# Long convolution and spectral mixing on one core: the Z of both sequences of a tick copied out of PSUM in one instruction

## The chip, the cores and the metric

The kernel runs on one core of a Trainium2 chip. A core has TensorE (PE in the profile; its weight loads are the row PEld), VectorE (DVE), ScalarE (ACT), GpSimd (POOL) and SyncE (SP, which here only starts DMAs). Each takes its own instructions in their order, and they wait for one another on semaphores. The metric is the device time of one execution in microseconds. Three runs of the kernel before took 392.10, 393.78 and 391.25 us, median 392.1. One execution was also profiled; its span from the first to the last instruction is 390.0 us, and every time of a single instruction is from it.

## The reference

Two operations, one behind the other. The first is a long convolution of x (8 sequences of 5696 positions, 128 channels) with a filter h per channel, by a Fourier transform of double length. The second transforms the result along the sequence, keeps 64 modes, mixes the channels of each mode with a complex matrix, transforms back, adds, and applies a channel matrix with a ReLU:

```python
    Xf = np.fft.rfft(x, n=L, axis=1)              # L = 2 * S
    Hf = np.fft.rfft(h, n=L, axis=0)
    y = np.fft.irfft(Xf * Hf[None, :, :], n=L, axis=1)[:, :S, :]
    ...
    X = np.fft.rfft(x, axis=1)                    # x is the y above
    Yr = np.einsum('bmd,mde->bme', Xr, w_r) - np.einsum('bmd,mde->bme', Xi, w_i)
    Yi = np.einsum('bmd,mde->bme', Xr, w_i) + np.einsum('bmd,mde->bme', Xi, w_r)
    Y[:, :n_modes] = Yr + 1j * Yi
    y = np.fft.irfft(Y, n=S, axis=1)
    u = x + y
    return (u + np.maximum(u @ w_ch, 0.0)).astype(np.float32)
```

## The kernel before

**Stages.** The transform of length 2·5696 is split in two: first over 89 points (90 frequencies k), then over 64. The 8 sequences are worked on in 4 groups of two. For each group `a_tile` (32 tiles) makes the first transform, and PE's matmuls `ps<-F,Xin` are its rows. Then come the *ticks*: 23 of them, each with four frequencies k (the last with two), so four blocks of 128 channels, or 512 columns, for each of the two sequences. After the four groups a last part goes back to positions, mixes the modes and writes the output. In the profiled execution the ticks of group 0 take place at some 46 to 96 us, those of group 1 at 112 to 151, of group 2 at 167 to 207 and of group 3 at 222 to 265, with the first transforms between them; the last part fills the rest.

**One tick** (function `tick`) of group `g_` at time t has these steps, each for another tick's data:

- `second(g_, t)`: the transform over 64 points, 16 small matmuls (`ps<-As,M`), into two neighbouring PSUM banks, one per sequence. Two such pairs of banks, 0 and 1 or 2 and 3, take turns.
- `products(g_, t)`: the product with the filter's transform (tile Hs), on DVE, into one of three buffers U. As a rule ACT first copies both banks to SBUF as fp16 (`copied`, rows `Xs<-ps`, 1024 columns; two buffers), and DVE multiplies from there (`U<-Xs,Hs`). In a *straight* tick DVE reads PSUM itself (`U<-ps,Hs`) and ACT's copy falls away.
- Z of tick t − 2 (`LC` = 2): four matmuls of 512 columns (`ps<-U,Wc`), two for each sequence b, the second adding to the first in the same bank. Then ACT copies each bank to the fp16 tile Zs or Zt, with the two sequences interleaved block by block, and SP writes the tile to DRAM (`zscr<-Zs`).
- G of tick t − 3 (`LM` = 3): eight small matmuls that read Zs (`ps<-G,Zs`) and add up the 64 modes in bank 7.
- in group 0 alone `filter_tick(t + 6)`: 16 matmuls (`ps<-Ah,M`) for the filter's own transform into banks 2 and 3, a copy of them to Hs, and two DMAs by SP that swap the halves of its partitions (`Hs<-Hs`). The product six ticks later needs them.

**Order on PE.** In group 0 a tick is: second stage, Z, G, filter. In groups 1 to 3 ticks go in pairs, an odd t and the next even one (`twin`): the second stages of both, Z, G, then Z and G of the even tick. Ticks 0 to 2 are the start; the pairs are (1, 2), (3, 4) ... (21, 22), and Z is there from tick 2. The last Z's fall in ticks 23 and 24, which have no second stage. In groups 0 to 2 the first tiles of the next group's `a_tile` stand between the steps of ticks 22 to 25 (`border`); in group 3 nothing does. Copies of x to their place for the next group (`x_place`, row `Xin<-Xt` on DVE) and the loads for them (`x_load`, POOL) are also made in the ticks of groups 0 to 2.

**Order on ACT.** An Xs copy and the Z copies in turn, as the ticks name them. In a pair with a straight product it is Xs of the even tick, then the Z copies of both ticks behind one another.

**Who waits for whom.** The order of all instructions is the program's; a recorder (`R.add`) derives the waits from tokens. `("bank", i)` is one of them: a matmul into a bank waits for the copy that read it last, and a copy waits for the last matmul into each bank that it reads. A copy that reads two banks waits for both, and both are free only when it has ended. Z's banks are 4, 5 and 6 in turn (`ZBANK`, by `turns`), one per sequence: 4 and 5, 6 and 4, 5 and 6, and so on. The filter copy's engine is chosen in `filter_tick`: ACT for ticks 0 to 5 except 2, DVE else.

Of the kernel before, what the change touches and what calls it, by code (L numbers as in the profile page):

```python
# [4 lines left out]
P = 128  # L5
# [118 lines left out]
def bass_long_conv_fft__then__afno_spectral_mix_kernel(nc, x, h, moe_w_r, moe_w_i, moe_w_ch, out):  # L124
    B, S, D = x.shape
# [72 lines left out]
    zs = nc.dram_tensor("zscr", [NP * NK * P, 2 * D], F16, kind="Internal")  # L198
# [7 lines left out]
    def at(name, cols, dt, off):  # L206
        return nc.alloc_sbuf_tensor_at(name, [P, cols], dt, offset=off)
# [21 lines left out]
    NU, NXS, NZ, NZX = 3, 2, 6, 10  # L229
# [14 lines left out]
    z_s = [at(f"Zs{i}", 1024, F16, a_st + NU * 4096 + (NXS + i) * 2048) for i in range(NZ)] + \  # L244
# [37 lines left out]
    def ap(t, row, p0, n, off, dims):  # L282
        return bass.AP(t, p0 * row + off, [[row, n]] + [list(d) for d in dims])
# [5 lines left out]
    def pv(bank, off, dims, p0=0, n=P):  # L289
        return bass.AP(ps, p0 * 4096 + bank * 512 + off, [[4096, n]] + [list(d) for d in dims])  # L290
# [5 lines left out]
    def bank(i):  # L296
        return ("bank", i)
# [3 lines left out]
    def evac(dst, src, reads, writes, scale=None, eng=None, after=()):  # L301
        e = eng
        if e is None:
            turn[0] ^= 1
            e = "scalar" if turn[0] else "vector"
        if e == "scalar":
            if scale is None:
                R.add(e, lambda h_: h_.copy(dst, src), reads, writes, after=after)  # L308
            else:
                R.add(e, lambda h_: h_.activation(dst, src, COPY, scale=scale), reads, writes, after=after)  # L310
        elif scale is None:
            R.add(e, lambda h_: h_.tensor_copy(dst, src), reads, writes, after=after)  # L312
        else:
            R.add(e, lambda h_: h_.tensor_scalar_mul(dst, src, scale), reads, writes, after=after)  # L314

    def dma(eng, dst, src, ring, reads=(), writes=(), after=()):
        R.add(eng, lambda h_: h_.dma_start(dst, src), reads, writes, ring=ring, after=after)  # L317

    def mm(o, l, r, st, sp, reads, writes):
        R.add("tensor", lambda h_: h_.matmul(o, l, r, start=st, stop=sp), reads, writes)  # L320
# [3 lines left out]
    def once(key, toks):  # L324
        if key in first:
            return []
        first[key] = 1
        return list(toks)
# [3 lines left out]
    def turns(name, items):  # L332
        i = ring2.get(name, 0)
        ring2[name] = i + 1
        return items[i % len(items)]
# [24 lines left out]
    def x_place(i, src, toks):  # L360
        R.add("vector", lambda e: e.tensor_copy(bass.AP(x_sb, i * XN * XS, [[XW, NQ], [XS, XN], [1, D]]),  # L361
                                                src),
              list(toks) + XZ, [("xin", i)])
# [38 lines left out]
    def mtok(k):  # L402
        t = [("m", k // KP)]
        if k % KP == KP - 1 and k < NK - 1:
            t.append(("m", k // KP + 1))
        return t

    W1, W2, WI = wc_sb[:, 0:P], wc_sb[:, P:2 * P], wi_sb[:, :]
    XSLOT = [0, 2]
    ZBANK = [4, 5, 6]  # L410
    MB = 7
    WARM = 92

# [9 lines left out]
    for j in range(16):  # L423
        t = turns("h", [0, 2, 4])
# [5 lines left out]
        for i in range(4 if j < 15 else 26):  # L430
# [4 lines left out]
             eng="vector" if j in (3, 7) else "scalar")  # L435
# [25 lines left out]
    def filter_tick(t, banks):  # L461
        n = len(ticks[t])
        hb = banks
        for i, k in enumerate(ticks[t]):
            for r in range(2):
                for dh in range(2):
                    mm(pv(hb[dh], i * DH, [[1, DH]]),
                       ap(m_sb, MW, J * dh, J, k * 3 * J + (J if r == 0 else 0) + dh * J, [[1, P]]),
                       ap(ah_sb, HW, J * dh, J, (2 * k + r) * DH, [[1, DH]]), r == 0, r == 1,
                       AHT + mtok(k) + [("ag", k)], [bank(hb[dh])])  # L470
        lo, hi = KT * t * D, (KT * t + n) * D
        old = once("xr", [t_ for r_ in XR for t_ in r_]) if t == 0 else []
        evac(h_sb[:, lo:hi], pv(hb[0], 0, [[DH, n], [512, 2], [1, DH]]), [bank(hb[0]), bank(hb[1])], [("h", t, 0)],
             eng="scalar" if t < LH and t != 2 else "vector",
             after=old)
        for p0, p1 in ((0, J), (J, 0)):
            dma("sync", h_sb[p0:p0 + J, HW + lo:HW + hi], h_sb[p1:p1 + J, lo:hi], "s", [("h", t, 0)], [("h", t, 1, p0)])
        if t % 2 and t // 2 < NG:
            s0, s1 = t // 2 * GP, min(t // 2 * GP + GP, NS)
            dma("sync", g_sb[:, s0 * P:s1 * P], bass.AP(c_g, s0 * P, [[GW, P], [1, (s1 - s0) * P]]), "c", (),  # L480
                [("g", t // 2)], after=[("ag", k) for k in range(s0, s1)])
# [66 lines left out]
    LC, LM, LH = 2, 3, 6  # L548
# [3 lines left out]
    def with_h_at(g_, t):  # L552
        return g_ == 0 and t + LH < NT
# [10 lines left out]
    def twin(g_, t):  # L564
        return g_ > 0 and t % 2 == 1

    def straight(g_, t):
        return g_ > 0 and t % 4 == 3

    def slot_of(g_, t):  # L570
        if g_ == 0 or t == 0:
# [38 lines left out]
    Z_OLD = [("ag", k) for k in range(NS, NS + 8 * (NZX - NZ))]  # L610
# [5 lines left out]
    def xtok(n):  # L616
        return [("xt", n, p_) for p_ in range(2)]

    def tick(g_, t):
        if g_ + 1 < NP:  # L620
            for i in range(2 * XC):
                if t == XPLACE[g_ > 0][i]:
                    x_place(i, bass.AP(x_st[i], 0, [[XB, NQ], [D, XN], [1, D]]), xtok(i))
        with_h = with_h_at(g_, t)
        if t < NT:
            of_two = t > 0 and twin(g_, t - 1)
            if not of_two:
                second(g_, t)
            products(g_, t, slot_of(g_, t))
            if twin(g_, t):  # L630
                second(g_, t + 1)
                if straight(g_, t):
                    copied(g_, t + 1, slot_of(g_, t + 1))
        drain = list(border[t]) if t in border and g_ + 1 < NP else []
        if drain and t >= NT:
            j, sl, e = drain.pop(0)
            a_tile(j, [sl], e)
        if g_ + 1 < NP and t % 2 == 0 and 0 < t <= 4 * XC:
            i = t // 2 - 1
            x_load(g_ + 1, i, x_st[i], xtok(i), [("u", t % NU)] + AST)  # L640
        if LC <= t < NT + LC:
            s_ = t - LC
            n = len(ticks[s_])
            i, zi = s_ % NU, zroom(g_, s_)
            zb = [turns("z", ZBANK) for b in range(2)]
            for b in range(2):
                for r in range(2):
                    mm(pv(zb[b], 0, [[1, n * D]]), (W1, W2)[r], u_s[i][:, r * 1024 + b * 512:r * 1024 + b * 512 + n * D],
                       r == 0, r == 1, [("u", i), ("wc",)], [bank(zb[b])])
                evac(bass.AP(z_s[zi], b * D, [[1024, P], [2 * D, n], [1, D]]),  # L650
                     pv(zb[b], 0, [[D, n], [1, D]]), [bank(zb[b])], [("zs", zi, b)], eng="scalar",
                     after=once(("zx", zi, b), Z_OLD) if zi >= NZ else ())
            zo = (g_ * NK + KT * s_) * P * 256
            dma("sync", bass.AP(zs, zo, [[256, P], [P * 256, n], [1, 256]]),
                bass.AP(z_s[zi], 0, [[1024, P], [256, n], [1, 256]]), "z",
                [("zs", zi, 0), ("zs", zi, 1)], [("zd", g_, s_)])
            if drain and t >= NT:
                j, sl, e = drain.pop(0)
                a_tile(j, [sl], e)
        if LM <= t < NT + LM:  # L660
            s_ = t - LM
            zi = zroom(g_, s_)
            for i, k in sorted(enumerate(ticks[s_]), key=lambda q: (s_ > 0 or q[1] != 1, q)):
                for b in range(2):
                    if k % 2:
                        o, off, n, sl = pv(MB, b * P, [[1, P]]), (k + 1) // 2 * P, P, (k + 1) // 2
                    else:
                        ms, off = even[k]
                        n, sl = 2 * len(ms), 0
                        dims = [[M, 2]] if len(ms) == 1 else [[ms[1] - ms[0], 2], [M, 2]]  # L670
                        o = pv(MB, b * P + ms[0], dims)
                    mm(o, z_s[zi][:, i * 256 + b * P:i * 256 + b * P + P], g_sb[:, off:off + n],
                       k == 1 and b == 0, k == NK - 1 and b == 1, [("g", sl // GP), ("zs", zi, b)], [bank(MB)])
        if drain and t < NT + LM - 1:
            j, sl, e = drain.pop(0)
            a_tile(j, [sl], e)
        if with_h:
            filter_tick(t + LH, [2, 3])
# [98 lines left out]
    for hb in range(2):  # L777
        evac(bass.AP(y_sb, hb * 32 * B, [[2 * M * B, P], [B, 32], [M * B, 2], [1, B]]),
             pv(6 + hb, 0, [[2 * B, 32], [B, 2], [1, B]]), [bank(6 + hb)], [("y", hb)], eng="vector" if hb else "scalar",
             after=ZY)  # L780
# [114 lines left out]
```

## Time and profile before

| | |
|---|---|
| runs | 391.25, 392.10, 393.78 us |
| span of the profiled execution | 390.0 us |
| instructions on PE, DVE, ACT | 5346, 346, 489 |
| Z matmuls of 512 columns | 352, mean 381 ns |
| Z copies of 512 columns on ACT (Zs / Zt) | 128 of 608 ns / 48 of 621 ns |
| Xs copies of 1024 columns on ACT | 69, mean 1019 ns |
| products from Xs / straight, on DVE | 69 of 1222 ns / 15 of 2283 ns |
| filter copies on DVE / ACT | 17 of 683 ns / 5 of 579 ns |

The busy shares in forty equal slices (tenths) and the granted clock of TensorE:

```profile
PE   7699999998989999989998989999999999999992
...
DVE  3358789988998999998998997875437767777784
ACT  8278689888889998989996999995457676777783
...
PEclk9899999999999999999999999998899999999997
```

A slice is 9.75 us. Matmuls overlap one another in the rows, since each is shown from its start to the arrival of its last result. So the pace of PE is read from start to start and not from their lengths. The rows of ACT and DVE overlap a little too where instructions follow at once.

### The profile page before, as it was taken

What the parts mean: (1) busy time and instruction counts of PE and PEld (TensorE: products, weight loads), DVE (VectorE), ACT (ScalarE), POOL (GpSimd) and SP (SyncE); (2) the same over time, 40 slices, a digit from 0 to 9 for tenths busy, and PEclk for the clock granted to TensorE, in tenths of its full rate; (3) what the DMA queues carried; (4) which work ended last, traced back from release to release, by engine and by line L of the source; (5) the groups of instructions that cost most, each with busy time, mean ns of one, the idle gap of its engine ahead of it and who ended that gap; (6) DMA issues with size and microseconds to landing.
All of it is one profiled execution on the core that took longest, in us unless ns stands there. A gap on an engine that the chain in (4) does not pass through costs nothing.

```text
span 390.0 us, 12484 instructions
## 1 busy us (share of the span) xinstructions
PE 363.7 (93%) x5346; PEld 280.4 (72%) x5346; DVE 304.9 (78%) x346; ACT 311.0 (80%) x489; POOL 84.3 (22%) x134
## 2 busy tenths in 40 slices
PE   7699999998989999989998989999999999999992
PEld 7597766654866666866666856668898988988871
DVE  3358789988998999998998997875437767777784
ACT  8278689888889998989996999995457676777783
POOL 8500013220453320643210411319300000000000
PEclk9899999999999999999999999998899999999997
DMA  7998559999598998999996849999999999999967
GB/s 146 184 284 327 143 98 257 272 253 281 93 138 188 225 254 235 98 129 198 226 260 193 86 134 383 301 337 394 405 400 394 418 405 409 405 406 379 360 276 287
DMA packets 87089, 103.94 MB, mean 267 GB/s; under 512 B 22823, under 2 KB 72615, under 8 KB 83563
## 3 DMA queue, kind: packets, MB, share of 16 engines
q1 hardware_dynamic: 62523, 67.73, 49.7%
q0 software_dynamic: 24512, 35.43, 43.5%
q8 instruction: 42, 0.69, 0.7%
q14 instruction: 12, 0.10, 0.1%
HBM read 70.61 MB, written 51.12 MB: 312 GB/s over the span
## 4 chain that ended last, share of the span: by engine, by line
PE 68%; DMA 9%; DVE 8%; ACT 8%; issue 3%; POOL 1%; SPq 0%; DVEq 0%; ACTq 0%; POOLq 0%
PE ps L320 68%; DMA Hin<-in_h_dram 3%; DVE As L314 2%; DMA Hs<-Hs 2%; DMA zscr<-Zs 2%; DMA Xt<-in_x_dram 2%; ACT As L310 2%; DVE U L599 2%; ACT Zs L308 1%; DVE U L607 1%; ACT Xs L308 1%; ACT R L829 1%; ACT Zt L308 1%; ACT UT L308 1%; DVE Hs L312 1%
## 5 line engine op out<-in xcount | busy, mean ns | idle before, releaser
L607 DVE TENSOR_TENSOR U<-Xs,Hs 128x2048 f16<-128x2048 f16 (+1 forms) x73 | 86.9, 1193 | 16.0 <-ACT Xs L308 11.3
L320 PE MATMUL ps<-U,Wc 128*128 128x512 f16 (+1 forms) x368 | 94.3, 376 | 1.2 <-DVE U L607 0.6
L308 ACT CAST Xs<-ps 128x1024 f16<-128x1024 f32 (+1 forms) x77 | 74.9, 977 | 12.3 <-PE ps L320 7.4
L308 ACT CAST Zs<-ps 128x512 f16<-128x512 f32 (+1 forms) x134 | 70.7, 597 | 4.1 <-PE ps L320 2.5
L830 DVE TENSOR_TENSOR O<-ps,R 128x512 f32<-128x512 f32 x81 | 52.5, 684 | 19.9 <-ACT R L829 12.5
L314 DVE TENSOR_SCALAR As<-ps 128x720 f16<-128x720 f32 x70 | 58.1, 884 | 6.7 <-PE ps L320 5.9
L829 ACT ACTIVATE R<-ps 128x512 f32<-128x512 f32 x96 | 50.9, 573 | 14.1 <-PE ps L320 13.7
L320 PE MATMUL ps<-F,Xin 128*128 128x180 f16 x512 | 53.8, 249 | 4.1 <-DVE Xin L361 1.9
L320 PE MATMUL ps<-As,M 64*128 64x128 f16 x1440 | 50.3, 217 | 4.5 <-DVE U L599 2.9
L320 PEld LDWEIGHTS ps<-F,Xin 128*128 128x128 f16 x512 | 44.5, 155 | 12.8 <-DVE As L314 3.6
L320 PE MATMUL ps<-WI,UT 128*128 128x256 f16 x360 | 51.8, 279 | 0.5 <-DVE O L830 0.4
L310 ACT ACTIVATE As<-ps 128x720 f16<-128x720 f32 (+1 forms) x61 | 45.8, 770 | 7.0 <-PE ps L320 5.7
L320 PEld LDWEIGHTS ps<-U,Wc 128*128 128x128 f16 x368 | 28.4, 97 | 30.7 <-ACT Zs L308 5.3
L317 POOL DMA_DIRECT2D Xt<-in_x_dram x48 | 25.9, 544 | 105.2 <-PE ps L320 100.3
L320 PEld LDWEIGHTS ps<-As,M 64*128 64x128 f16 x1440 | 40.6, 94 | 10.7 <-DVE U L599 3.6
L308 ACT CAST UT<-ps 128x712 f16<-128x712 f32 x40 | 30.0, 752 | 19.0 <-PE ps L320 18.1
L320 PEld LDWEIGHTS ps<-WI,UT 128*128 128x128 f16 x360 | 39.3, 152 | 4.2 <-issue 1.7
L320 PE MATMUL ps<-IBs,C 128*128 128x356 f16 x128 | 40.5, 326 | 0.6
L320 PEld LDWEIGHTS ps<-G,Zs 128*128 128x128 f16 x524 | 26.6, 96 | 15.0 <-ACT Zs L308 2.5
L607 DVE TENSOR_TENSOR U<-ps,Hs 128x2048 f16<-128x2048 f32 x15 | 34.2, 2283 | 0.0
L320 PE MATMUL ps<-G,Zs 128*128 128x128 f16 (+2 forms) x524 | 33.0, 192 | 0.1
L312 DVE CAST UT<-ps 128x712 f16<-128x712 f32 x24 | 21.4, 890 | 9.8 <-PE ps L320 9.8
(87 smaller groups left out, 510.4 us busy)
## 6 DMA issues: line engine op xcount, KB each, us to landing
out_dram<-O SPq DMA_DIRECT2D x39, 512.0 KB, 10.2
zscr<-Zs SPq DMA_DIRECT2D x64, 256.0 KB, 7.4
Xt<-in_x_dram POOLq DMA_DIRECT2D x24, 320.0 KB, 7.0
zscr<-Zt SPq DMA_DIRECT2D x24, 256.0 KB, 6.9
W<-wscr POOLq DMA_DIRECT2D x4, 1024.0 KB, 8.0
M<-cM POOLq DMA_DIRECT2D x5, 720.0 KB, 20.5
ZT0a<-zscr SPq DMA_DIRECT2D x3, 1024.0 KB, 13.1
Hs<-Hs SPq DMA_DIRECT2D x44, 64.0 KB, 5.9
```

Source lines behind the costliest of these rows:

```text
L308: R.add(e, lambda h_: h_.copy(dst, src), reads, writes, after=after)
L310: R.add(e, lambda h_: h_.activation(dst, src, COPY, scale=scale), reads, writes, after=after)
L312: R.add(e, lambda h_: h_.tensor_copy(dst, src), reads, writes, after=after)
L314: R.add(e, lambda h_: h_.tensor_scalar_mul(dst, src, scale), reads, writes, after=after)
L317: R.add(eng, lambda h_: h_.dma_start(dst, src), reads, writes, ring=ring, after=after)
L320: R.add("tensor", lambda h_: h_.matmul(o, l, r, start=st, stop=sp), reads, writes)
L599: R.add("vector", lambda e, b=b, s_=s_: e.tensor_tensor(bass.AP(u_s[i], b * 512, [[2048, P], [1024, 2], [1, n * D]]), s_, hv, MULT), [tok, ...
L607: R.add("vector", lambda e: e.tensor_tensor(uv, src, hv, MULT), bk + [("h", t, 0), ("h", t, 1, 0), ("h", t, 1, J)], [("u", i)])
L829: R.add("scalar", lambda e: e.activation(rv, src_r, RELU), bk, [("r", i % NR)], after=once(("r", i % NR), G_ALL + XTT + [("y", 0), ("y", 1 ...
L830: R.add("vector", lambda e: e.tensor_tensor(ov, src_u, rv, ADD), bk + [("r", i % NR)], [key + (h_,)], after=once(key, old))
```

## The change

It has three parts.

1. In `tick` the two Z copies of a tick become one ACT instruction of 1024 columns (2 × 4 × 128) that reads both banks and writes the tile with both sequences interleaved, as before. The banks are now 4 or 6 in turn for the first sequence (`ZBANK`), and always 5 for the second (`ZB1`). The matmuls and their order are the same.
2. `straight` no longer holds at t = 3: in groups 1 to 3 tick 3 has an Xs copy on ACT and a product from it. Of five straight products in a group four are left (ticks 7, 11, 15, 19).
3. The filter copies of ticks 9, 15 and 21 go from DVE to ACT.

ACT has 92 Z copies fewer (92 of 1024 columns or, in the last tick of a group, 512, where there were 184), and three Xs copies and three filter copies more. DVE has three filter copies fewer and as many products as before; PE and SP have the same instructions in the same order.

```diff
-    ZBANK = [4, 5, 6]
+    ZBANK, ZB1 = [4, 6], 5
...
-             eng="scalar" if t < LH and t != 2 else "vector",
+             eng="scalar" if (t < LH and t != 2) or t in (9, 15, 21) else "vector",
...
     def straight(g_, t):
-        return g_ > 0 and t % 4 == 3
+        return g_ > 0 and t % 4 == 3 and t > 3
...
-            zb = [turns("z", ZBANK) for b in range(2)]
+            zb = [turns("z", ZBANK), ZB1]
             for b in range(2):
                 for r in range(2):
                     mm(pv(zb[b], 0, [[1, n * D]]), (W1, W2)[r], u_s[i][:, r * 1024 + b * 512:r * 1024 + b * 512 + n * D],
                        r == 0, r == 1, [("u", i), ("wc",)], [bank(zb[b])])
-                evac(bass.AP(z_s[zi], b * D, [[1024, P], [2 * D, n], [1, D]]),
-                     pv(zb[b], 0, [[D, n], [1, D]]), [bank(zb[b])], [("zs", zi, b)], eng="scalar",
-                     after=once(("zx", zi, b), Z_OLD) if zi >= NZ else ())
+            zk = [("zs", zi, b) for b in range(2)]
+            evac(bass.AP(z_s[zi], 0, [[1024, P], [D, 2], [2 * D, n], [1, D]]),
+                 pv(zb[0], 0, [[(zb[1] - zb[0]) * 512, 2], [D, n], [1, D]]), [bank(q) for q in zb], zk, eng="scalar",
+                 after=once(("zx", zi), Z_OLD) if zi >= NZ else ())
```

## The prediction

> **What bounds the kernel now.** I read the page first: its sum of busy time, its forty slices, its chain that ended last.
>
> ```profile
> PE 363.7 (93%) x5346; PEld 280.4 (72%) x5346; DVE 304.9 (78%) x346; ACT 311.0 (80%) x489; POOL 84.3 (22%) x134
> ...
> PE 68%; DMA 9%; DVE 8%; ACT 8%; issue 3%; POOL 1%; SPq 0%; DVEq 0%; ACTq 0%; POOLq 0%
> ```
>
> PE is the longest and carries 68% of the chain, but ACT is at 80% over the whole span, so the stage that the change touches has to be read by itself. The second view is the busy time of each engine in stretches (us, then busy us of PE, PEld, DVE, ACT, POOL, the granted clock, DMA share, GB/s).
>
> ```profile
> 120.00:130.00 10.00, 10.00 (x158) 6.37 (x152) 8.57 (x8) 9.86 (x16) 3.12 (x6) 1.00 1.00 204
> ...
> 222.40:232.00 9.60, 8.37 (x153) 5.74 (x154) 8.71 (x8) 8.06 (x13) 1.07 (x2) 1.00 0.28 74
> 232.00:242.00 10.00, 10.00 (x158) 6.47 (x158) 7.34 (x7) 9.86 (x17) 1.06 (x2) 1.00 1.05 367
> ```
>
> In the ticks of groups 1 to 3, PE and ACT are both full. Busy shares can't say which of them waits. So the third view is the timeline of two tick pairs of group 1, (7, 8) and (9, 10), engine by engine (start, length, line; the bracket is idle time before it).
>
> ```profile
> 122.81 1.07 PE L320 MATMUL ps<-As,M 64*128 64x128 f16 x32
> 123.81 1.04 PE L320 MATMUL ps<-U,Wc 128*128 128x512 f16 x4
> 124.69 0.49 PE L320 MATMUL ps<-G,Zs 128*128 128x2 f16 x8
> 125.01 1.07 PE L320 MATMUL ps<-U,Wc 128*128 128x512 f16 x4
> 125.92 0.52 PE L320 MATMUL ps<-G,Zs 128*128 128x2 f16 x8
> 126.37 1.07 PE L320 MATMUL ps<-As,M 64*128 64x128 f16 x32
> ```
>
> ```profile
> 125.47 0.11 PEld L320 LDWEIGHTS ps<-U,Wc 128*128 128x128 f16 x2 [0.36 <-ACT Zs L308]
> ```
>
> ```profile
> 123.92 1.01 ACT L308 CAST Xs<-ps 128x1024 f16<-128x1024 f32 x1
> 124.83 1.08 ACT L308 CAST Zs<-ps 128x512 f16<-128x512 f32 x2
> 125.78 1.11 ACT L308 CAST Zt<-ps 128x512 f16<-128x512 f32 x2
> 127.03 1.01 ACT L308 CAST Xs<-ps 128x1024 f16<-128x1024 f32 x1
> ```
>
> From start to start on PE, a pair is: both ticks' second stage 1.00 us, Z 0.88, G 0.32, Z 0.91, G 0.45, together 3.56. The next pair, which begins at 126.37 and ends at 129.85, takes 3.48 with the same instructions (1.00, 0.87, 0.33, 0.86, 0.42). The 0.08 between them is PE's wait for bank copies, seen in the PEld line: the third Z matmul waits for a bank that ACT is still copying, and most of that wait lies behind running matmuls. The nine pairs of ticks 3 to 20 run from 115.77 to 147.49, 3.52 us each. So PE is within 0.04 us per pair of having no wait at all. ACT looks full only because it has just enough work. PE sets the pace, and ACT's time costs only where it holds a bank that PE needs.
>
> **One copy for both sequences.** The copy of 1024 columns isn't in the trace in this form (two banks in, two interleaved halves out). The nearest row is the Xs copy, 1024 columns out of two adjacent banks: 1019 ns. Two Z copies one behind the other end 1.08 us after the first begins (124.83). From the next start, an Xs copy holds ACT for only 0.91 (123.92 to 124.83). I take 1.02, with 0.91 and 1.08 as ends of the range. ACT saves about 0.1 us per tick by it.
>
> What matters is what the copy now waits for and who waits for it. It can start only when all four Z matmuls are done (before: after two). And every tick's third Z matmul writes bank 5, so it waits for the whole copy of the tick before. With three banks in turn it waited for a single 512-column copy, begun earlier. Work it out for one pair, PE's second stage starting at 0:
>
> - Z of the first tick starts at 1.00; the four matmuls last 1.04, so their result is there at 2.04.
> - ACT starts about 0.05 after a result: at 71.62 sixteen second-stage matmuls of 0.61 end at 72.23, and the waiting Xs copy starts at 72.28. So the copy runs from 2.09 to 3.11. ACT is free then: an Xs copy that starts at 0.66, or at 1.11 in a pair with a straight product, has given ACT free after 0.91.
> - PE has meanwhile done the first G (to 2.20) and the first half of the second Z (0.43, to 2.63). Its third matmul follows the copy by 0.04 (the copy of 124.83 lasts 0.60; the weights load starts at 125.47): 3.15.
> - The second half of Z takes 0.43 and the second G 0.42: the pair ends at 4.00.
>
> So PE stands still for 0.52 us once per pair, and behind that matmul is queued everything else of PE's: its Z, the G, the next pair's second stage, hence the Xs copies and the products. Between an even tick and the next odd one nothing waits: G, two second stages and half a Z are 0.42 + 1.00 + 0.43 of PE, and the copy, started at most 0.2 us later because ACT does an Xs copy first, ends sooner. A pair costs 4.00 − 3.52 = 0.48 us. There are ten pairs per group (ticks 3 to 22): 4.8 us in each of groups 1, 2 and 3.
>
> Corrections at the ends of groups. In group 1 the first tile of the next group waits 0.33 us for its x on DVE (at 151.15), in group 2 1.12 us (207.35), the latter for a load issued six ticks earlier, which three pairs (1.4 us) of slower ticks cover. Both go: 4.5 and 3.7 us. In those groups ticks 23 and 24 have other tiles' matmuls between their Z's, and nothing is added. Group 3 has none:
>
> ```profile
> 261.08 1.03 PE L320 MATMUL ps<-U,Wc 128*128 128x512 f16 x4
> 261.95 0.49 PE L320 MATMUL ps<-G,Zs 128*128 128x4 f16 x8
> 262.27 1.13 PE L320 MATMUL ps<-U,Wc 128*128 128x512 f16 x4
> 263.24 0.52 PE L320 MATMUL ps<-G,Zs 128*128 128x4 f16 x8
> 263.60 0.60 PE L320 MATMUL ps<-U,Wc 128*128 128x256 f16 x4
> ```
>
> There the Z's of the last three ticks follow one another with only a G between. The step from one third matmul to the next becomes 0.61 (half a Z with its drain) + 0.05 + 1.02 + 0.05 = 1.73 us, where it was 1.19 to 1.3. Twice some 0.5, and the last short Z and G wait for copies of 1.02 and about 0.6 with little else to do: I take 1.4 for these ticks. Group 3: 6.2 us.
>
> In group 0 a tick has filter matmuls or at least a second stage between two Z's: at 72.17 to 74.25 one tick takes 2.08 us on PE, and without the filter (0.24) 1.84. Both exceed 1.73, so the wait for bank 5 is hidden there; the cover of the last six ticks is only 0.1 us.
>
> **One straight product fewer.** At tick 3 of groups 1 to 3 a Xs copy (0.91 of ACT) and a product from it (1222 ns) replace one of 2283 ns on DVE. ACT would be busy 7 × 0.95 of the 8.0 us that two pairs then take, and DVE isn't late at tick 3. Nothing on the path, either way.
>
> **Three filter copies on ACT.** Those of ticks 9, 15 and 21, made in ticks 3, 9 and 15 of group 0, leave DVE (683 ns each) and cost ACT 579 ns each, between a Z copy and the next Xs copy, which they delay by about 0.3 us; its product is needed by PE two ticks later. The swap DMAs behind them keep their place in SP's queue and start up to 0.6 us earlier. PE waits for a filter copy on DVE twice, 0.22 us at 71.38 and 0.33 at 75.94; DVE is relieved of one copy just before. I take a gain of 0.3, between 0 and 0.55. The other waits of group 0 (ACT 1.05 and 0.60 us for zscr, products waiting for swaps) are for DMA, and stay.
>
> **Sum.** 4.5 + 3.7 + 6.2 − 0.3 = 14.1 us on the span of 390.0. The median of the runs is 2.1 above that span, so 406.2, rounded 406. From 266 us on nothing is changed; that part is moved as a whole.
>
> **Rivals.** *ACT was the limit, and its shorter queue wins.* For it: 9.86 of 10 busy, and 0.1 us less per tick. Then every pair takes PE's 3.48 (30 × 0.04 = 1.2), and the waits of 0.33, 1.12 and 0.55 go: 386.8, or 388.9 as a median. It decides only if bank 5 is free again before PE wants it: 1.19 − 0.61 − 0.10 = 0.48 us after the copy starts, and a copy of half the columns takes 608 ns. Chance 6%: 2% for something more than this (below 388.2), 4% inside 1%.
>
> *The clock falls.* PE would stand still for 0.52 of 4.00 us, 13%. The trace shows a stretch like that at full clock: 222.4 to 232, PE busy 87%, clock 1.00. It also shows one low window, 6.9 us at a mean of 0.51 (269.3 to 276.2), during matmuls of few columns. One such window per group, in which half of PE's 87% is lost, is 3.0 us each, so 415. [...] Chance 7%.
>
> *The copy over two banks doesn't pipeline* and costs two single ones, 1.22: 0.20 × 30 = 6 more, 412. Against it: the Xs row. 7%.
>
> **Numbers.** The forecast has 80%. About 1% (3.9 us) is what measurement can tell from no change. Low end: a copy of 0.91 takes 0.11 × 30 = 3.3 off, group 0 and the scatter of the runs about 1 more: 401.5. High end: 1.08 adds 1.8, a second low window of 3.4 us in the last part, whose place in time shifts, about 1.7, so with the slow copy's lower part 411.5. Faster 0.02, same 0.04, slower 0.94.
>
> **What would show it.** In groups 1 to 3: pairs of 4.0 us on PE, with one gap of about 0.5 before the third matmul of the second Z, ended by ACT; Z copies of about 1.02; ACT below full. Wrong: pairs at 3.5 with no such gap, or the copy starting before the fourth matmul ends; or a clock below 1.00 in the ticks.

## The result and the profile after

The changed kernel takes 405.25 us (402.38 to 406.99, 4 runs), the kernel before 392.94 (391.25 to 395.89, 4 runs). The ratio, estimated from all of these runs, is 1.029 with a 95% interval of 1.022 to 1.035 (the two medians alone would give 1.031). The profiled execution has a span of 403.5 us, 13.5 more than before. On its page the first line is busy time, the second the chain that ended last:

```profile
PE 367.2 (91%) x5346; PEld 278.5 (69%) x5346; DVE 299.3 (74%) x343; ACT 311.4 (77%) x403; POOL 83.6 (21%) x134
...
PE 70%; ACT 14%; DVE 6%; DMA 6%; issue 2%; POOL 1%; SPq 0%; DVEq 0%; ACTq 0%; POOLq 0%
```

ACT does 92 instructions fewer for Z and has as much busy time as before (311.4 against 311.0 us; three Xs copies and three filter copies came to it), and its part of the chain went from 8% to 14%. That is the pattern to notice: an engine that isn't busier holds more of the chain, because others now wait for it. The busy time of the engines in a stretch of group 1's ticks says the same (columns as in the prediction):

```profile
120.00:130.00 10.00, 9.30 (x148) 5.75 (x142) 7.83 (x7) 8.45 (x10) 3.12 (x6) 1.00 1.02 198
```

Neither PE nor ACT is full any more: 10.00 and 9.86 became 9.30 and 8.45. They take turns in waiting for each other. The timeline of the pair (7, 8) of group 1, engine by engine, shows where:

```profile
123.54 1.07 PE L320 MATMUL ps<-As,M 64*128 64x128 f16 x32
124.54 1.04 PE L320 MATMUL ps<-U,Wc 128*128 128x512 f16 x4
125.41 0.49 PE L320 MATMUL ps<-G,Zs 128*128 128x2 f16 x8
125.73 0.59 PE L320 MATMUL ps<-U,Wc 128*128 128x512 f16 x2
126.68 0.60 PE L320 MATMUL ps<-U,Wc 128*128 128x512 f16 x2 [0.35 <-ACT Zs L308]
127.12 0.49 PE L320 MATMUL ps<-G,Zs 128*128 128x2 f16 x8
127.54 1.07 PE L320 MATMUL ps<-As,M 64*128 64x128 f16 x32
```

```profile
126.67 0.11 PEld L320 LDWEIGHTS ps<-U,Wc 128*128 128x128 f16 x2 [0.84 <-ACT Zs L308]
```

```profile
124.64 1.01 ACT L308 CAST Xs<-ps 128x1024 f16<-128x1024 f32 x1 [0.19 <-PE ps L320]
125.61 1.01 ACT L308 CAST Zs<-ps 128x1024 f16<-128x1024 f32 x1
127.32 1.01 ACT L308 CAST Zt<-ps 128x1024 f16<-128x1024 f32 x1 [0.70 <-PE ps L320]
```

The second Z is torn in two. Its third matmul starts at 126.68, 0.06 us after the joined copy of the first Z has ended (125.61 + 1.01). Without a wait it would have started 0.43 after 125.73. So PE stands still for 0.52 us; the bracket shows only 0.35, because the last matmul's result is still under way for a part of that time, until 126.32 (125.73 + 0.59). The next copy in turn waits 0.70 us for PE. The pair takes 4.00 us, where it took 3.56 or 3.48.

The waits of PE's weight loads for Z copies, over the whole execution (total us, times, longest), before and after:

```profile
PEld ps L320 <- ACT Zs L308: 7.8, 29, 0.6
...
PEld ps L320 <- ACT Zt L308: 2.8, 11, 0.4
```

```profile
PEld ps L320 <- ACT Zs L308: 21.7, 29, 1.1
...
PEld ps L320 <- ACT Zt L308: 9.7, 13, 0.8
```

The end of group 3 after, to be put beside the five lines of before:

```profile
274.55 0.49 PE L320 MATMUL ps<-G,Zs 128*128 128x4 f16 x8
274.88 0.59 PE L320 MATMUL ps<-U,Wc 128*128 128x512 f16 x2
275.82 0.61 PE L320 MATMUL ps<-U,Wc 128*128 128x512 f16 x2 [0.35 <-ACT Zs L308]
276.26 0.49 PE L320 MATMUL ps<-G,Zs 128*128 128x4 f16 x8
276.59 0.38 PE L320 MATMUL ps<-U,Wc 128*128 128x256 f16 x2
277.53 0.39 PE L320 MATMUL ps<-U,Wc 128*128 128x256 f16 x2 [0.56 <-ACT Zs L308]
...
278.60 0.34 PE L320 MATMUL ps<-G,Zt 128*128 128x4 f16 x4 [0.35 <-ACT Zt L308]
```

Each Z stops in its middle, and the last G waits once more.

Where the 13.5 us are is read from the starts of matmuls in the timeline: the first second-stage matmul (A), the first tile of the next group behind each group's ticks (B1 to B3), the first matmul of the modes (C).

| stretch | before, us | after, us | difference | forecast |
|---|---|---|---|---|
| start to A | 46.45 | 46.56 | +0.1 | 0 |
| A to B1: ticks of group 0 | 49.29 | 48.86 | −0.4 | −0.3 |
| B1 to B2: tiles and ticks of group 1 | 55.40 | 59.83 | +4.4 | +4.5 |
| B2 to B3: group 2 | 56.20 | 59.81 | +3.6 | +3.7 |
| B3 to C: group 3 | 58.70 | 64.79 | +6.1 | +6.2 |
| C to the end | 123.93 | 123.62 | −0.3 | 0 |

### The profile page after: what moved, and what is told of

The parts are those of the page before. It is cut to its first block, busy times and chain, and to the rows that moved or that the text cites. A ratio compares the mean times of both kernels' runs of the same rounds, so it can differ in the third digit from the quotient of the medians.

```text
span 403.5 us, 12407 instructions
## 1 busy us (share of the span) xinstructions
PE 367.2 (91%) x5346; PEld 278.5 (69%) x5346; DVE 299.3 (74%) x343; ACT 311.4 (77%) x403; POOL 83.6 (21%) x134
## 3 DMA queue, kind: packets, MB, share of 16 engines
q1 hardware_dynamic: 62523, 67.73, 47.9%
## 4 chain that ended last, share of the span: by engine, by line
PE 70%; ACT 14%; DVE 6%; DMA 6%; issue 2%; POOL 1%; SPq 0%; DVEq 0%; ACTq 0%; POOLq 0%
PE ps L320 69%; ACT Zs L308 6%; DMA Hs<-Hs 3%; ACT Zt L308 3%; DMA Hin<-in_h_dram 3%; DVE As L314 2%; ACT As L310 2%; DVE U L599 2%; ACT R L830 1%; ACT UT L308 1%; POOL Hin L317 1%; ACT Xs L308 1%; DVE Hs L312 0%; SPq L317 0%; DVE UT L312 0%
## 5 line engine op out<-in xcount | busy, mean ns | idle before, releaser
L607 DVE TENSOR_TENSOR U<-Xs,Hs 128x2048 f16<-128x2048 f16 x76 | 90.8, 1195 | 32.8 <-ACT Xs L308 23.5
L320 PE MATMUL ps<-U,Wc 128*128 128x512 f16 (+1 forms) x368 | 99.5, 377 | 12.6 <-ACT Zs L308 8.5
L308 ACT CAST Xs<-ps 128x1024 f16<-128x1024 f32 (+1 forms) x80 | 77.9, 978 | 11.4 <-PE ps L320 8.9
L308 ACT CAST Zs<-ps 128x1024 f16<-128x1024 f32 (+1 forms) x67 | 67.0, 999 | 12.7 <-PE ps L320 8.6
L320 PEld LDWEIGHTS ps<-U,Wc 128*128 128x128 f16 x368 | 26.9, 97 | 48.7 <-ACT Zs L308 21.7
L308 ACT CAST Zt<-ps 128x1024 f16<-128x1024 f32 (+1 forms) x25 | 25.1, 1003 | 7.7 <-PE ps L320 6.7
```

The lines of the kernel that those rows point to most:

```text
L607: R.add("vector", lambda e: e.tensor_tensor(uv, src, hv, MULT), bk + [("h", t, 0), ("h", t, 1, 0), ("h", t, 1, J)], [("u", i)])
```

## The experiments

The theory: in the ticks of groups 1 to 3 PE sets the pace, and it stands still once per pair until the joined copy of 1024 columns has ended, since every Z needs bank 5. The rivals: the copies that parts 2 and 3 put on ACT cost the time; or the joined copy costs by itself, wherever it stands. The fixed bank and the joining are two parts of one edit and were taken apart as well.

All runs at a glance. Stretches are those of the table above; the ratio is to the kernel before, with its 95% interval.

| run | span | group 0 | group 1 | group 2 | group 3 | C to end | ratio |
|---|---|---|---|---|---|---|---|
| before | 390.0 | 49.3 | 55.4 | 56.2 | 58.7 | 123.9 | 1 |
| the change | 403.5 | 48.9 | 59.8 | 59.8 | 64.8 | 123.6 | 1.029 [1.022, 1.035] |
| 1: parts 2 and 3 | 388.8 | 48.0 | 55.8 | 56.5 | 59.1 | 123.2 | 1.001 [0.997, 1.005] |
| 2: bank 5, two copies | 398.5 | 49.3 | 58.3 | 58.3 | 62.2 | 122.8 | 1.019 [1.015, 1.024] |
| 3: bank 5 first | 417.3 | 49.5 | 64.6 | 64.6 | 70.2 | 122.1 | 1.069 [1.063, 1.075] |
| 4: no pairs, joined | 394.3 | 47.9 | 57.8 | 57.8 | 62.5 | 122.1 | 1.016 [1.010, 1.022] |
| 5: no pairs, two copies | 395.9 | 48.6 | 57.9 | 57.9 | 61.2 | 123.9 | 1.018 [1.009, 1.027] |
| 6: joined where covered | 389.5 | 47.9 | 56.1 | 56.7 | 59.4 | 123.0 | 1.004 [1.001, 1.008] |
| 7: joined in group 0 | 392.3 | 50.1 | 55.4 | 56.1 | 59.1 | 125.4 | 1.002 [0.998, 1.005] |
| 8: as 6, straight tick 3 | 388.3 | 46.7 | 55.7 | 55.9 | 59.0 | 123.3 | 1.001 [0.998, 1.005] |

The last column of stretches is the same program in all ten, and it still spreads from 122.1 to 125.4 us; group 0 has one and the same program in the change and in runs 4, 6, 7 and 8, and takes 46.7 to 50.1. Groups 1 to 3 repeat better: run 7 has the ticks of the kernel before there, and differs by 0.02, 0.08 and 0.36 us. So an edit in groups 1 to 3 is read from their own stretches, and 1 us in the span of one execution is read as nothing.

**Run 1: parts 2 and 3 alone** (against the kernel before).

```diff
-             eng="scalar" if t < LH and t != 2 else "vector",
+             eng="scalar" if (t < LH and t != 2) or t in (9, 15, 21) else "vector",
...
-        return g_ > 0 and t % 4 == 3
+        return g_ > 0 and t % 4 == 3 and t > 3
```

> The kernel before with parts 2 and 3 of the change alone (no straight product at tick 3, three filter copies on ACT); Z keeps its two copies and three banks. Theory (PE waits for bank 5 until the copy of 1024 columns has ended): these parts are off the path, pairs stay at 3.5 us, span 389.0 to 390.3, ratio to before 0.997 to 1.001. Rival (the three additional Xs copies and filter copies load ACT, which is full in the ticks): a good part of the 13.5 us is here, span above 393.

388.8 us, 0.2 below the expected range, and ratio 1.001. The rival falls: the loss isn't in parts 2 and 3. But a pair shows what the prediction had called free. The pair (3, 4) takes 3.92 us here, 3.56 in the kernel before, with PE's second stage of the pair (5, 6) waiting for an Xs copy:

```profile
118.03 1.07 PE L320 MATMUL ps<-As,M 64*128 64x128 f16 x32 [0.37 <-ACT Xs L308]
```

**Run 2: bank 5 fixed, but two copies** (against the changed kernel, as runs 3, 4 and 6 are).

```diff
+                evac(bass.AP(z_s[zi], b * D, [[1024, P], [2 * D, n], [1, D]]),
+                     pv(zb[b], 0, [[D, n], [1, D]]), [bank(zb[b])], [("zs", zi, b)], eng="scalar",
+                     after=once(("zx", zi, b), Z_OLD) if zi >= NZ else ())
-            zk = [("zs", zi, b) for b in range(2)]
-            evac(bass.AP(z_s[zi], 0, [[1024, P], [D, 2], [2 * D, n], [1, D]]),
-                 pv(zb[0], 0, [[(zb[1] - zb[0]) * 512, 2], [D, n], [1, D]]), [bank(q) for q in zb], zk, eng="scalar",
-                 after=once(("zx", zi), Z_OLD) if zi >= NZ else ())
```

> The changed kernel, but Z leaves in two copies of 512 columns again; the banks stay 4 or 6, and 5. It parts the cost of the fixed bank from the cost of the joined copy. Theory, by the rows of before: without a straight product the first copy starts at 1.66 in the pair, the second ends at 2.75, the third matmul of the next Z starts at 2.80, pair 3.65; with a straight product an Xs copy stands ahead on ACT, the second copy ends at 3.16 and the pair takes 4.05. Six and four such pairs per group: 3.81 on average, span about 397 (395.5 to 398.5). Rival (the fixed bank is the whole of it, joining costs nothing): span 403 as with the change. Rival (joining is the whole of it): span 390.

398.5 us, at the upper edge; the pairs are 3.63 without and 4.02 with a straight product, as worked out (3.65, 4.05), the first two 3.92 and 3.74. PE's lines of a straight pair, then ACT's:

```profile
126.67 0.59 PE L320 MATMUL ps<-U,Wc 128*128 128x512 f16 x2
127.63 0.61 PE L320 MATMUL ps<-U,Wc 128*128 128x512 f16 x2 [0.36 <-ACT Zs L308]
```

```profile
125.58 1.01 ACT L308 CAST Xs<-ps 128x1024 f16<-128x1024 f32 x1
126.49 1.08 ACT L308 CAST Zs<-ps 128x512 f16<-128x512 f32 x2
```

The two copies stand behind an Xs copy, and the second ends at 127.57, as late as a joined one would. Without that Xs copy the first copy starts before all four matmuls are done (in the next pair at 130.13, where the last result of the four comes at 130.53), and the pair is only 0.15 us longer than with three banks (3.63 against 3.48). So neither rival holds alone. The mean of the nine full pairs is 3.85 us, against 3.57 in run 1, which has part 2 as well, and 4.01 with the change: taken apart in this order, the fixed bank is 0.28 and the joining 0.16.

**Run 3: the shared bank first.**

```diff
-            zb = [turns("z", ZBANK), ZB1]
+            zb = [ZB1, turns("z", ZBANK)]
```

> The changed kernel with the two banks of a Z swapped: bank 5 for the first sequence, 4 or 6 in turn for the second. The copy and the order are the same; the wait for bank 5 moves from the third matmul of a Z to the first. Theory: half a Z (0.43 us) less cover per pair, the stop is 0.96 instead of 0.53, pairs of 4.45, 13 us more in groups 1 to 3, about 1 at the end of group 3 and 1 to 3 in group 0, where a tick of 2.08 or 1.84 is shorter than the loop of 2.16: span 418 to 421. Rival (the joined copy costs by itself, on ACT): span 403.5, as with the change.

417.3 us. The pairs take 4.43, worked out as 4.45: the same copy, 0.43 us less cover, 0.43 us more per pair. The whole Z now waits:

```profile
127.03 0.49 PE L320 MATMUL ps<-G,Zs 128*128 128x2 f16 x8
128.30 1.04 PE L320 MATMUL ps<-U,Wc 128*128 128x512 f16 x4 [0.78 <-ACT Zs L308]
```

The pair of ticks 3 and 4 takes 4.61. Groups 1 to 3 are 15.0 us longer than with the change, where the expectation makes 14 of it. The span is below the range all the same, because group 0 was 0.7 us longer and not 1 to 3, and the last part 1.5 shorter. In group 0 the stop is there: most of its ticks take 2.14 us or more, where the loop was worked out as 2.16. But the same stretch with the change holds other waits of up to 0.78 us, which hide a part of the difference. The rival (403.5) falls. It is the place of the wait that counts, not the copy.

**Runs 4 and 5: a second stage between any two Z's**, with the joined copy and with two copies in three banks.

```diff
     def twin(g_, t):
-        return g_ > 0 and t % 2 == 1
+        return False
...
-        return XSLOT[((t - 1) // 4 + t) % 2]
+        return XSLOT[(t + 1) % 2]
```

Run 4 makes this edit in the changed kernel, run 5 in the kernel of run 1, which has two copies and three banks. The second part of the edit lets the two bank pairs of the second stage take turns from tick to tick.

> The changed kernel without pairs: in groups 1 to 3 every tick is second stage, Z, G, so that between two Z's there is always a second stage. Theory: a tick takes PE 1.84 to 1.85, more than the loop of 1.73 through the copy, the stop before the third matmul is gone, two ticks take 3.70; only the end of group 3 keeps its stops: span 394 to 396. Rival (the joined copy costs wherever it stands, 0.5 us per two ticks): 4.0 or more per two ticks, span 403 or more.

> No pairs as in the run before, but Z with two copies and three banks in turn, as in the kernel before; parts 2 and 3 are in. Theory: PE's 1.84 to 1.85 per tick sets the pace here too, so joining the copies neither costs nor saves where PE has 1.73 us of other work between two Z's: groups 1 and 2 within 0.5 us of the run without pairs and with the joined copy, group 3 about 1.5 shorter at its end, span 393 to 394.5. Rival (the joined copy costs wherever it stands): 390 or less.

With the joined copy a tick of groups 1 to 3 from tick 4 on takes 1.85 us, and its Z is not torn (PE's timeline of run 4):

```profile
124.19 0.62 PE L320 MATMUL ps<-As,M 64*128 64x128 f16 x16
124.74 1.04 PE L320 MATMUL ps<-U,Wc 128*128 128x512 f16 x4
125.62 0.49 PE L320 MATMUL ps<-G,Zs 128*128 128x2 f16 x8
126.03 0.62 PE L320 MATMUL ps<-As,M 64*128 64x128 f16 x16
```

The span is 394.3, within the range and 9 us less than with the change, with the same copies. A part of that is luck. In groups 1 to 3 it is 6.3 us less; the rest lies in the start, group 0 and the last part, which don't repeat. The profiled execution is also the shortest of the four: the others have spans of 396.9 to 398.5, above the range. One thing that the expectation left out is tick 3, which takes 2.45 us because Z waits 0.40 us for a product. Two copies in run 5 make groups 1 and 2 0.1 us longer and group 3 1.35 shorter at its end, also as expected. Its span of 395.9 missed the range of 393 to 394.5, through the two stretches that don't repeat: group 0 is 0.7 longer than in run 4, the last part 1.9. Joined or not makes no difference where PE has 1.73 us of other work between two Z's: nearly every tick takes 1.85 us in both. Without pairs both are slower than the kernel before, since PE needs 1.85 us per tick where pairs need 1.76, and because of tick 3.

**Run 6: joined only where it is covered**, in group 0 and for even Z's up to 18 of the other groups. Where `one` holds, a Z has the joined copy, else the two of the kernel before.

```diff
+            if g_ > 0:
+                zb = {21: [4, 6], 22: [5, 4]}.get(s_, [6, 5] if s_ % 2 == 0 else [5, 4])
+            one = g_ == 0 or (s_ % 2 == 0 and s_ < 20)
...
```

> Parts 2 and 3, and pairs as before. Z is joined to one copy in group 0 (banks 4 or 6, and 5) and for the even Z's of groups 1 to 3 up to 18 (banks 6 and 5), behind which PE has G, two second stages and more; the odd ones keep two copies (banks 5 and 4), so the even Z's second half, into bank 5, waits for a copy of 512 columns alone. Theory: no stop of more than 0.1 us, pairs of 3.48 to 3.56 as before, span 388.8 to 390.3, ratio to before 0.996 to 1.001. Rival (the joined copy costs wherever it stands): half of the loss is here, span about 396.

```profile
125.43 1.07 PE L320 MATMUL ps<-As,M 64*128 64x128 f16 x32
126.43 1.04 PE L320 MATMUL ps<-U,Wc 128*128 128x512 f16 x4
127.31 0.49 PE L320 MATMUL ps<-G,Zt 128*128 128x2 f16 x8
127.63 1.02 PE L320 MATMUL ps<-U,Wc 128*128 128x512 f16 x4
128.49 0.49 PE L320 MATMUL ps<-G,Zt 128*128 128x2 f16 x8
128.91 1.07 PE L320 MATMUL ps<-As,M 64*128 64x128 f16 x32
130.04 1.04 PE L320 MATMUL ps<-U,Wc 128*128 128x512 f16 x4
```

```profile
128.94 1.04 ACT L308 CAST Zt<-ps 128x1024 f16<-128x1024 f32 x1
```

389.5 us, and pairs of 3.48 and 3.60. At the start of a group two pairs, (3, 4) and (7, 8), take 3.98 and 3.65, more than the expected 3.48 to 3.56. About half of the Z's are joined (53 of 92) and the loss of 13.5 us is gone. The ratio of 1.004 lies above the expected range by 0.003. Part 2 is a piece of that, as run 8 shows. Another is that the cover falls just short in a pair with a straight product: the joined copy at 128.94 stands behind an Xs copy and ends at 129.98, and the next Z starts at 130.04, 1.13 us after its pair began and not 1.00.

**Runs 7 and 8: a try at something faster than both.** Run 7 joins in group 0 alone and keeps the straight product of tick 3; run 8 is run 6 with that product kept.

Run 8 against run 6:

```diff
     def straight(g_, t):
-        return g_ > 0 and t % 4 == 3 and t > 3
+        return g_ > 0 and t % 4 == 3
```

Run 7 against run 8:

```diff
-                zb = {21: [4, 6], 22: [5, 4]}.get(s_, [6, 5] if s_ % 2 == 0 else [5, 4])
-            one = g_ == 0 or (s_ % 2 == 0 and s_ < 20)
+                zb = [[4, 5], [6, 4], [5, 6]][s_ % 3]
+            one = g_ == 0
```

> The kernel before with the joined copy in group 0 alone, where a tick covers the loop, and the three filter copies on ACT; straight products and the two copies with three banks in groups 1 to 3 are those of before. Theory: ticks of groups 1 to 3 as before (pair of ticks 3 and 4 at 3.56, the others 3.48 and 3.56); the last ticks of group 0 go from 1.90 to 1.85; span 388.0 to 389.8, ratio to before 0.994 to 1.000, not above 1.003. Rival (the joined copy costs by itself): 5 us more in group 0.

> As the run with the joined copy where it is covered, but with the straight product at tick 3 kept, so that the two differ in part 2 alone. Theory: the pair of ticks 3 and 4 goes from 3.98 back to about 3.6, so 0.4 us less in each of groups 1 to 3, 1.2 in all; the other pairs stay at 3.48 and 3.60. Span 388.0 to 389.5. Rival (the 0.4 is from the start of the group and not from part 2): the pair stays at 3.98.

Run 8 settles part 2. The pair (3, 4) goes from 3.98 to 3.65, and groups 1 and 3 are 0.37 and 0.39 us shorter. Group 2 is 0.82 shorter, but 0.43 of that is a shorter wait for x at its end (0.47 us in place of 0.90). Run 7 has the pairs of before. Its span of 392.3 missed the range through group 0 (50.1) and the last part (125.4), and its ratio of 1.002 the range up to 1.000. Neither is faster than the kernel before: 1.002 and 1.001, with 1 in both intervals. PE had a wait of at most 0.08 us per pair to give.

Not tried: the joined copy with banks 4, 5 and 6 in turn. Two Z's in a row have one bank in common there too, and it is always the second bank of the later Z. So by the order of the program its third matmul would wait for the whole joined copy just the same, and the shares of 0.28 and 0.16 hold only for the order in which run 2 takes the two apart.

## Why the prediction was right

**PE and not ACT sets the pace.** It was read from the pitch of matmuls, 3.52 us per pair with 0.04 of waiting, against a view in which ACT looked full. The rival by which ACT was the limit, with pairs of 3.48, is out. Runs 4 and 6 bear out that PE sets the pace: it follows PE's own work and waits, whether ACT has an instruction more or less.

**The loop through bank 5.** Forecast for a pair: copy from 2.09 to 3.11, third matmul at 3.15, end at 4.00. In the pair above it is 2.07 to 3.08, 3.14 and 4.00. At the end of group 3 the step from one third matmul to the next was forecast as 1.73 and is 1.71 (275.82 to 277.53). The joined copy, which no row of before showed, takes what the Xs copy takes:

```profile
L308 ACT CAST Zs<-ps 128x1024 f16<-128x1024 f32 x64 | 65.2, 1019 | 12.7 <-PE ps L320 8.6 <-DMA zscr<-Zs 3.8
```

The rival of 1.22 us is out.

**The ends of groups.** The two waits for x, 0.33 and 1.12 us, are gone: in both groups the next group's first tile now starts 0.33 us behind the start of the G before it, where it was 0.82 and 1.61. That is 0.49 and 1.28 us less, 0.16 more than the idle time in the brackets by which they were forecast, since a bracket starts only when the last result is there. The two groups came out 0.1 us under the forecast each. From the second stage of tick 21 to the first matmul behind the last G, group 3 needs 7.58 us (271.19 to 278.77) where it needed 5.86; the 1.7 more had been put at 0.5 for the pair and 1.4 for the rest.

**Part 2, nothing on the path.** Right for the changed kernel, where the pair (3, 4) takes 4.06 at most and the others 4.00. The likely cover is the stop itself: ACT has time in hand there, as the 0.70 us for which it waits for PE in the pair above show. In runs 1 and 6, without the stop, part 2 costs about 0.4 us in each of the three groups. The prediction named ACT's slack in the slower pairs as the cover, but not what happens without it.

**Part 3.** It isn't shown. In the trace of the change the two waits for filter copies that it named are gone: those ticks take 2.10 and 2.08 us where they took 2.36 and 2.48. But a wait of 0.25 us for another filter copy on DVE has come (at 80.23), and in runs 2, 5, 6 and 7, which have part 3 too, waits for a filter copy stand at the same place in the ticks again, 0.17 to 0.66 us each. That group 0 came out at −0.4 where −0.3 was forecast is luck: the same program takes 46.7 to 50.1 us there.

**What it overlooked in group 0.** The cover there was said to hide bank 5. It does where ACT copies at once: the Z at 90.34 runs through, behind a copy that started at 89.67 without a wait. Where ACT waits for a write to DRAM before it copies, the wait now reaches PE in the middle of a Z, as at 88.93 with 0.65 us of idle time; the copy before it had waited 0.75 us for zscr. Run 7, whose group 0 is the longest, has two such stops, of 0.40 and 1.17 us; ACT's copies at 85.39 and 88.58 had waited 0.47 and 1.26 us for zscr there. They are one of the waits by which group 0 varies, and their share wasn't measured apart.

**The clock.** The rival with low windows in the ticks did not come: the stretch above has 1.00. The high end of the forecast's range counted a second low window of 3.4 us in the last part. That was an estimate, and the runs don't show the term: behind C the traces of the kernel before and of the change both have one window of 6.83 us, and one at the very end, in which PE has no work.

## What to carry to other kernels

Two copies out of PSUM were also two releases in this kernel. Before joining such copies, write down for each bank when its next writer wants it, and compare the loop (last result, start of the copy, its length, release, rest of the next writer) with the other work that the writer's engine has between the two; here 1.73 us against 1.19, and 0.5 us lost each time. Where the other work was longer than the loop, joining was free but gained nothing, since PE set the pace (in runs 4 and 5 nearly every tick takes 1.85 us, joined or not). Which engine that was showed in the pitch of its instructions (3.52 us per pair on PE, with 0.04 of waiting) and not in its busy share (ACT with 9.86 of 10 us).

## What the runs showed of the hardware

Frequent short stops of PE didn't lower its clock here. In run 3 PE stands still for 0.95 of 4.43 us again and again (from the end of a G at 127.35 to 128.30, for one); a stretch of it in group 1:

```profile
120.00:130.00 10.00, 8.44 (x139) 5.49 (x138) 7.61 (x6) 7.76 (x9) 2.17 (x5) 1.00 1.02 181
```

The granted clock is 1.00 in it and in another stretch of the same run, 256 to 266 us, with PE standing still for 21% of a pair. It is 1.00 too in the ticks of the kernel before (49 to 265 us, with the first transforms between them) and of the change (49 to 278).

The traces of the kernel before and of the change each have three low windows, with a granted clock of 0.50. The first lies before the ticks and lasts 3.41 us in both (from 16.7 and from 15.9 us). The second lies shortly behind the start of the last part and lasts 6.83 us in both (from 269.3 and from 282.1). In the kernel before it begins among matmuls of 16 and 89 columns, and in the 3.5 us ahead of it PE has no gap above 0.2 us. The third begins 4.6 and 5.3 us before the end, where PE has no work left. What brings the windows on wasn't shown. In all ten profiled executions the mean clock of the whole span is 0.976 to 0.994.

These windows can be a part of the scatter from execution to execution: of run 4's four, the shortest has the highest mean clock (394.3 us, 0.994) and the longest the lowest (398.5 us, 0.981). They are not the whole of it: of run 1's ten, the shortest and the longest have nearly the same (388.8 us with 0.985, 393.9 with 0.983). How much of the 122.1 to 125.4 us of the last part they make was not settled: that of run 3 is among the shortest, with a low clock in it too, 0.81 from 303 to 309 us.
